# Spectral mixing with a gated causal unit on one core: set-up reordered, the filter worked up in four parts, the first batch loaded by two queues

## Chip, cores, metric

One core of one Trainium2 chip, one program of 11040 instructions, no loop left at run time. The metric is the device time of one execution in microseconds (us). Before the change it is 417.4 us, the median of three runs (417.29 to 417.82).

## What is computed

The reference, cut to its core. `x` is (8, 3200, 256) float32, the filter (1601, 256) in a real and an imaginary part, `K` is 5.

```python
X = np.fft.rfft(x, axis=1)
F = (filt_r + 1j * filt_i)[None, :, :]
y = np.fft.irfft(X * F, n=3200, axis=1)
...
xp = np.concatenate([zeros(B, K - 1, D), y], axis=1)
gate_pre = sum(conv_w[k] * xp[:, k:k + S, :] for k in range(K))
gate = 1.0 / (1.0 + np.exp(-gate_pre))
out = (gate * (y @ w_val)) @ w_out
```

## The kernel before

**The transform.** A sequence of 3200 is taken as 128 x 25 (L = 128, R = 25), and both directions are matrix products on TensorE. The 256 channels are cut into 52 groups of five (the last overlaps its neighbour), since 25 x 5 = 125 fills the partitions. The groups are cut into eight chunks of 6 or 7 (`CH`, NF = 8). With 8 batches there are 64 chunks, and one step G of the main loop (L496) starts one of them: step G runs the first stage of chunk G, and later stages of earlier chunks.

**The stages of a chunk.** `permute` (L95) reorders the chunk's channels from the loaded batch `xb` into `xpb`: on ScalarE (L105), or for odd chunks of batches 1 and later on GpSimd (L103). `s1` (L343) multiplies with the 128-point table `cf_t` on TensorE (L348), and VectorE copies the result to `sob` (L351). `s2` (L354), one step later, multiplies with the 25-point tables (L360 to L363), ScalarE copies to `xsb` (L365), and VectorE multiplies with the worked-up filter `fr_t`, `fm_t` (L376 to L379). `inva` (L383, two steps later still) starts the inverse. It is the last stage that works on chunks of groups.

**The stages of a batch.** From eleven steps after a batch's first chunk, `invb` (L403) finishes the inverse in seven pieces. With the first of them GpSimd copies a few columns of `yt` to the place where the causal convolution looks back (L423, L425). Two steps later `conv` (L427) runs the convolution as matmuls (L434) and needs that copy; `val` (L444) and `outp` (L462) follow, and SyncE (SP) stores the result (L478). So for batch 0: `s1` of chunk 13 and the first `conv` are in the same step, G = 13.

**Loading x.** `load_x(b, r)` (L81) loads residue r of batch b as float32 rows of 1 KB which the transfer turns into bf16. Because 3200 rows don't divide evenly it takes two transfers for each r but r = 0: 49 a batch, all issued by GpSimd (L88). Three buffers `xb` turn round. Batch 0 is issued in the set-up (L170), the others from a queue in the main loop (L485, L502): at step G the queue is worked off up to entry (G + 8) x 25/8, which at G = 0 is the whole of batch 1. Right behind it comes `load_w` (L506), eight transfers of the two weight matrices, and then batch 2. GpSimd's `permute` instructions and its `yt` copies stand in the same in-order stream, between those issues.

**Set-up (L109 to L324).** Tables are made by VectorE and ScalarE. SP issues four loads of the filter: `gd` (rows used as they are) and `gh` (rows that have to be reversed), for the real (i = 0) and the imaginary part (i = 1), then two small ones of `cw`, from which VectorE makes `dg_t` (L320). Then, first for i = 0 and after that for i = 1: `turn` copies `gd` into `gp` (L247 or L249); `gh` is reversed by float32 matmuls with `rev` (L262), three times two, and turned into `gp` as well; 52 matmuls (L272) with ScalarE or VectorE copies give `ft`; 50 matmuls for both parts together (25 each, L293) with copies (L307, L309, L310) fill `fr_t` and `fm_t`. All 52 groups go through each stage together. ScalarE does the copies of i = 0 up to `ft`, VectorE those of i = 1. The main loop's matmuls stand behind all of this in TensorE's order.

**Order.** The program fixes what depends on what. A planner orders each engine's instructions by the order in the program and by its own estimate of when inputs are there; on the chip each engine then works in that order and waits where an input is late. PSUM is four tiles, `ps`, that turn round over all of these stages.

Of the kernel before, what the change touches and what calls it, by code (L numbers as in the profile page):

```python
# [11 lines left out]
I32 = mybir.dt.int32  # L12
# [18 lines left out]
def kernel(  # L31
# [48 lines left out]

    def load_x(b, r):  # L81
        xt = xb[b % NX]
        na = min(L, -(-(S - L * r) // R))
        for a0, a1, s in ((0, na, L * r), (na, L, L * r + R * na - S)):
            if a1 > a0:
                src = bass.AP(tensor=x.tensor, offset=x.offset + (b * S + s) * D,
                              ap=[[R * D, a1 - a0], [1, D]])
                nc.gpsimd.dma_start(out=xt[a0:a1, r, :], in_=src)  # L88
# [6 lines left out]
    def permute(b, c):  # L95
        g0, nd = CH[c]
        xt = xb[b % NX]
        xp = xpb[(NF * b + c) % NP]
        for i0, i1, d0 in split(g0, nd):
            dst = xp[:, i0:i1, :].rearrange("p g (r j) -> p g r j", j=J)  # L100
            src = xt[:, :, d0:d0 + J * (i1 - i0)].rearrange("p r (g j) -> p g r j", j=J)
            if c % 2 and b > 0:
                nc.gpsimd.tensor_copy(dst, src)  # L103
            else:
                nc.scalar.activation(dst, src, AF.Copy)  # L105

    C2, S2, SN2 = (tb_t[0:P2, i].rearrange("p k j -> p (k j)") for i in (0, 1, 2))

    with tc.tile_pool(name="gen", bufs=1) as g1, tc.tile_pool(name="gen2", bufs=2) as g2:  # L109

        def floormod(src_ap, divisor):
            shp = list(src_ap.shape)
            divi = g2.tile(shp, I32, name=f"fm_i{shp[1]}")
            bak = g2.tile(shp, FP32, name=f"fm_b{shp[1]}")
            q = g2.tile(shp, FP32, name=f"fm_q{shp[1]}")
            cm = g2.tile(shp, FP32, name=f"fm_c{shp[1]}")
            nc.vector.tensor_scalar(divi[...], src_ap, 1.0 / float(divisor), None,
                                    op0=ALU.mult)
            nc.vector.tensor_copy(bak[...], divi[...])
            nc.vector.scalar_tensor_tensor(q[...], bak[...], -float(divisor), src_ap,  # L120
                                           op0=ALU.mult, op1=ALU.add)
            nc.vector.tensor_scalar(cm[...], q[...], float(divisor) - 0.5, None,
                                    op0=ALU.is_ge)
            nc.vector.scalar_tensor_tensor(q[...], cm[...], -float(divisor), q[...],
                                           op0=ALU.mult, op1=ALU.add)
            nc.vector.tensor_scalar(cm[...], q[...], -0.5, None, op0=ALU.is_lt)
            nc.vector.scalar_tensor_tensor(q[...], cm[...], float(divisor), q[...],
                                           op0=ALU.mult, op1=ALU.add)
            return q

        def iota(shape, pattern, base, cm, name):
            t = g1.tile(shape, FP32, name=name)
            nc.gpsimd.iota(t[...], pattern=pattern, base=base, channel_multiplier=cm,
                           allow_small_or_imprecise_dtypes=True)
            return t

        nc.vector.memset(b_npi[:, :], -PI)
        pcol = iota([128, 1], [[0, 1]], 0, 1, "pcol")
        kc = iota([128, 2, 64], [[-1, 2], [1, 64]], 1, 0, "kc")
        kt = iota([128, 2 * R], [[1, 2 * R]], 0, 0, "kt")  # L140
        kt65 = iota([128, 65], [[1, 65]], 0, 0, "kt65")
        q64 = iota([128, 1], [[0, 1]], 64, -1, "q64")
        ident = g1.tile([128, 128], FP32, name="ident")
        nc.vector.memset(ident[:, :], 1.0)
        nc.gpsimd.affine_select(out=ident[:, :], in_=ident[:, :], pattern=[[1, 128]],
                                compare_op=ALU.is_equal, fill=0.0, base=0,
                                channel_multiplier=-1)
        ac = g1.tile([128, 1], FP32, name="ac")
        nc.vector.memset(ac[...], 2.0)
        for i in (63, 64):  # L150
            nc.gpsimd.affine_select(out=ac[...], in_=ac[...], pattern=[[0, 1]],
                                    compare_op=ALU.not_equal, fill=1.0, base=-i,
                                    channel_multiplier=1)

        gd, gh, gp = [], [], []
        for i, f in enumerate((filt_r, filt_i)):
            g = g1.tile([65, 13, D], FP32, name=f"gd{i}")
            nc.sync.dma_start(
                out=g[...],
                in_=bass.AP(tensor=f.tensor, offset=f.offset,  # L160
                            ap=[[D, 65], [L * D, 13], [1, D]]))
            h = g1.tile([65, 12, D], FP32, name=f"gh{i}")
            nc.sync.dma_start(
                out=h[...],
                in_=bass.AP(tensor=f.tensor, offset=f.offset + 64 * D,
                            ap=[[D, 65], [L * D, 12], [1, D]]))
            gd.append(g)
            gh.append(h)
            gp.append(g1.tile([65, ND, R, J], BF16, name=f"gp{i}"))
        for r in range(R):  # L170
            load_x(0, r)
        for t in sob:
            nc.vector.memset(t[:, :, 0:1], 0.0)
            nc.vector.memset(t[:, :, SW - 1:SW], 0.0)
        for t in xsb:
            nc.vector.memset(t[:, :, :, 65:W], 0.0)

        pr = g1.tile([128, 128], FP32, name="pr")
        nc.vector.tensor_scalar(pr[...], kc[...].rearrange("p b k -> p (b k)"),
                                pcol[:, 0:1], None, op0=ALU.mult)  # L180
        nc.vector.tensor_scalar(pr[:, 0:65], pr[:, 0:65], 0.75 * L, None, op0=ALU.add)
        q = floormod(pr[...], L)
        nc.scalar.activation(cf_t[:, :], q[...], AF.Sin, bias=b_npi[:, 0:1],
                             scale=2.0 * PI / L)

        jp = g1.tile([128, 1], FP32, name="jp")
        nc.vector.tensor_copy(jp[...], floormod(pcol[...], J)[...])
        rp = g1.tile([128, 1], FP32, name="rp")
        nc.vector.tensor_tensor(rp[...], pcol[...], jp[...], op=ALU.subtract)
        nc.vector.tensor_scalar(rp[...], rp[...], 1.0 / J, None, op0=ALU.mult)  # L190
        mk = g1.tile([128, J], FP32, name="mk")
        nc.vector.tensor_scalar(mk[...], kt[:, 0:J], jp[:, 0:1], None, op0=ALU.is_equal)

        ph = g1.tile([128, 2 * R], FP32, name="ph")
        nc.vector.tensor_scalar(ph[:, 0:R], kt[:, 0:R], rp[:, 0:1], 4.0, op0=ALU.mult,
                                op1=ALU.mult)
        nc.vector.tensor_scalar(ph[:, R:2 * R], ph[:, 0:R], 3.0 * R, None, op0=ALU.add)
        qp = floormod(ph[...], 4 * R)
        sc = g1.tile([128, 2, R], FP32, name="sc")
        nc.scalar.activation(sc[...].rearrange("p c k -> p (c k)"), qp[...], AF.Sin,  # L200
                             bias=b_npi[:, 0:1], scale=2.0 * PI / (4 * R))

        def expand(dst, src, n):
            nc.vector.tensor_tensor(dst, src.unsqueeze(2).to_broadcast((128, n, J)),
                                    mk[...].unsqueeze(1).to_broadcast((128, n, J)),
                                    op=ALU.mult)

        expand(tb_t[:, 2], sc[:, 0], R)
        expand(tb_t[:, 0], sc[:, 1], R)
        nc.vector.tensor_scalar(tb_t[:, 1], tb_t[:, 2], -1.0, None, op0=ALU.mult)  # L210

        m3 = g1.tile([128, 1], FP32, name="m3")
        hi = g1.tile([128, 1], FP32, name="hi")
        nc.vector.tensor_scalar(hi[...], rp[...], 12.5, None, op0=ALU.is_ge)
        nc.vector.tensor_scalar(m3[...], rp[...], -2.0, 37.0, op0=ALU.mult, op1=ALU.add)
        nc.vector.tensor_tensor(m3[...], m3[...], hi[...], op=ALU.mult)
        nc.vector.tensor_tensor(m3[...], m3[...], rp[...], op=ALU.add)
        nc.vector.tensor_scalar(m3[...], m3[...], 3.0, None, op0=ALU.mult)
        m3q = floormod(m3[...], R)
        xr = g1.tile([128, 2, R], FP32, name="xr")  # L220
        for h in range(2):
            nc.vector.tensor_scalar(xr[:, h, :], kt[:, 0:R], m3q[:, 0:1], None,
                                    op0=ALU.is_equal)
# [332 lines left out]
```

## Time and profile before

| what | us |
|---|---|
| median of the runs | 417.4 |
| the profiled execution's own time | 416.61 |
| span of that execution | 414.9 |
| first `s1` matmul (L348) starts | 61.47 |
| `s1` of chunk 3 | 67.75 |
| `s1` of chunk 8 | 80.42 |
| first GpSimd `permute` (L103, chunk 9) | 88.97 |
| `s1` of chunk 9 | 89.95 |
| first `yt` copy on GpSimd (L423, L425) | 108.23 |
| first `conv` matmul (L434) | 109.33 |
| from one batch's `s1` to the next in the later batches | 40.3 |

Engine busy shares over the span: PE (TensorE matmul) 86%, DVE (VectorE) 73%, ACT (ScalarE) 66%, POOL (GpSimd) 60%. They average over a set-up, a start and a steady part that differ, so the stretches have to be read one by one: which wait ends last there. Starts are us from the span's start; an entry in brackets behind a timeline row is the time for which the engine sat idle before it, and what ended that.

### The profile page before, as it was taken

The numbers are of one execution on the slowest core, as the hardware profiler recorded it, in microseconds if no ns is written. First come the engines' busy times: TensorE is split into PE (matmuls) and PEld (weight loads), VectorE is DVE, ScalarE is ACT, GpSimd is POOL, SyncE is SP. The second block draws the span as 40 slices with busy tenths as digits, with TensorE's granted clock in tenths as the row PEclk, the third lists the DMA queues.
The fourth block names the chain that finished last, engine by engine and source line by source line (L and its number), as shares of the span: only waits on it lengthen the run. The fifth ranks groups of instructions, "written<-read, shape, count | busy, mean of one in ns | idle before, by whom it ended". The sixth has DMA issues, their size and how long they took to land.

```text
span 414.9 us, 11040 instructions
## 1 busy us (share of the span) xinstructions
PE 357.3 (86%) x4628; PEld 241.1 (58%) x4659; DVE 304.7 (73%) x465; ACT 274.4 (66%) x338; POOL 249.2 (60%) x471
## 2 busy tenths in 40 slices
PE   0688868938598999899999999999999999999994
PEld 0154466626366676667666756666766666666552
DVE  5235578948577798779977888788878887874454
ACT  2442246828567787778777877787778777766762
POOL 5599999899999998899994979210021002000000
PEclk9999999979699999999999999999999999999998
DMA  7976667556458766776683757231222122213334
GB/s 147 183 95 70 64 61 66 57 54 63 47 55 165 148 124 107 157 147 127 108 161 104 138 97 156 92 120 45 107 86 92 52 103 80 90 52 141 128 153 164
DMA packets 48951, 43.65 MB, mean 105 GB/s; under 512 B 12628, under 2 KB 41734, under 8 KB 48902
## 3 DMA queue, kind: packets, MB, share of 16 engines
q0 software_dynamic: 36224, 13.41, 31.5%
q1 hardware_dynamic: 12678, 29.55, 19.8%
q8 instruction: 36, 0.59, 0.6%
q14 instruction: 13, 0.11, 0.1%
HBM read 30.07 MB, written 26.21 MB: 136 GB/s over the span
## 4 chain that ended last, share of the span: by engine, by line
PE 52%; POOL 21%; DVE 13%; DMA 6%; issue 4%; ACT 3%; DVEq 0%; ACTq 0%; POOLq 0%
POOL xb L88 18%; PE ps L434 10%; PE ps L451 8%; PE ps L394 8%; PE ps L468 7%; DMA xb<-in_x_dram 6%; PE ps L416 5%; DVE o L473 4%; PE ps L348 4%; DVE za L376 2%; PE ps L360 2%; DVE zb L378 2%; PE ps L363 2%; PE ps L362 2%; PE ps L361 2%
## 5 line engine op out<-in xcount | busy, mean ns | idle before, releaser
L88 POOL DMA_DIRECT2D xb<-in_x_dram x392 | 203.9, 551 | 18.0 <-DMA xb<-in_x_dram 11.7
L439 ACT ACTIVATE gt<-ps 128x1024 bf16<-128x1024 f32 (+1 forms) x56 | 52.2, 933 | 60.4 <-PE ps L434 58.0
L456 DVE TENSOR_TENSOR gv<-ps,gt 128x1024 bf16<-128x1024 f32 (+1 forms) x56 | 62.1, 1109 | 37.9 <-PE ps L451 28.8
L351 DVE CAST sob<-ps 125x768 bf16<-125x768 f32 x64 | 65.4, 1022 | 29.7 <-PE ps L348 29.0
L103 POOL COPY xpb<-xb 128x875 bf16<-128x875 bf16 (+2 forms) x35 | 30.3, 869 | 72.1 <-PE ps L348 72.1
L434 PE MATMUL ps<-yt,dg_t 64*64 64x512 bf16 (+1 forms) x1120 | 66.6, 362 | 3.0 <-POOL yt L425 2.8
L365 ACT ACTIVATE xsb<-ps 125x780 bf16<-125x780 f32 x64 | 56.5, 883 | 15.0 <-PE ps L363 14.1
L394 PEld LDWEIGHTS <-z 125*64 125x64 bf16 x1664 | 49.9, 112 | 26.6 <-issue 25.7
L394 PE MATMUL ps<-tb_t,z 125*64 125x125 f16 x1664 | 60.7, 223 | 0.4 <-PE ps L363 0.4
L399 ACT ACTIVATE u<-ps 128x750 bf16<-128x750 f32 (+2 forms) x72 | 57.1, 793 | 2.8 <-PE ps L394 0.7
L418 ACT ACTIVATE yt<-ps 128x1024 bf16<-128x1024 f32 (+1 forms) x56 | 52.2, 932 | 4.5 <-PE ps L416 4.5
L468 PE MATMUL ps<-wo_t,gv 128*128 128x256 bf16 x400 | 52.8, 273 | 1.1 <-DVE gv L456 1.1
L451 PE MATMUL ps<-yt,wv_t 128*128 128x512 bf16 (+1 forms) x193 | 50.8, 352 | 1.9 <-DMA xb<-in_x_dram 0.3
L348 PE MATMUL ps<-cf_t,xpb 128*125 128x128 f16 x416 | 37.2, 231 | 14.9 <-POOL xpb L103 8.9
L468 PEld LDWEIGHTS <-gv 128*128 128x128 bf16 x400 | 38.9, 98 | 14.3 <-DVE gv L456 1.5
L376 DVE TENSOR_TENSOR za<-xsb,fr_t 125x792 bf16<-125x792 bf16 x64 | 40.4, 631 | 5.4 <-ACT xsb L365 4.7
L434 PEld LDWEIGHTS <-dg_t 64*64 64x64 bf16 x1120 | 28.4, 107 | 27.0 <-issue 14.5
L379 DVE TENSOR_TENSOR z<-za,zb 125x792 bf16<-125x792 bf16 x64 | 43.3, 676 | 1.1
L348 PEld LDWEIGHTS <-xpb 128*125 128x125 bf16 x416 | 32.0, 145 | 17.8 <-POOL xpb L103 9.4
L378 DVE TENSOR_TENSOR zb<-xsb,fm_t 125x792 bf16<-125x792 bf16 x64 | 40.5, 632 | 0.0
L416 PE MATMUL ps<-ci_t,u 128*128 128x128 f16 x400 | 33.4, 222 | 7.6 <-ACT u L399 7.1
L473 DVE COPY o<-ps 128x1024 f32<-128x1024 f32 (+1 forms) x32 | 36.8, 1150 | 2.3 <-PE ps L468 2.3
(92 smaller groups left out, 367.7 us busy)
## 6 DMA issues: line engine op xcount, KB each, us to landing
out_dram<-o SPq DMA_DIRECT2D x32, 512.0 KB, 3.1
out_dram<-o SPq DMA_DIRECT2D x24, 384.0 KB, 2.3
gd<-in_filt_r_dram SPq DMA_DIRECT2D x1, 845.0 KB
gd<-in_filt_i_dram SPq DMA_DIRECT2D x1, 845.0 KB
gh<-in_filt_r_dram SPq DMA_DIRECT2D x1, 780.0 KB
gh<-in_filt_i_dram SPq DMA_DIRECT2D x1, 780.0 KB
xb<-in_x_dram POOLq DMA_DIRECT2D x8, 64.0 KB, 2.8
xb<-in_x_dram POOLq DMA_DIRECT2D x8, 61.5 KB, 2.6
```

The source lines that it names most:

```text
L88: nc.gpsimd.dma_start(out=xt[a0:a1, r, :], in_=src)
L348: nc.tensor.matmul(ps[0:P2, 128 * i:128 * i + 128], lhsT=xp[:, i, :], rhs=cf_t[:, :], start=True, stop=True)
L351: nc.vector.tensor_copy(so[0:P2, 0:nd, 1:SW - 1], ps[0:P2, 0:nd * 128].rearrange("p (g k) -> p g k", g=nd))
L365: nc.scalar.activation(xs[0:P2, :, 0:nd, 0:65], ps[0:P2, :].rearrange("p (c n) -> p c n", c=2)[:, :, 0:65 * nd] .rearrange("p c (g k) -> p ...
L394: nc.tensor.matmul(ps[lo:lo + 64, o:o + P2], lhsT=z[0:P2, blk, i, s0:s0 + 64], rhs=tab, start=first, stop=not first)
L399: nc.scalar.activation(u[:, :, d0:d0 + J * (i1 - i0)].rearrange("p r (g j) -> p r g j", j=J), pv[:, i0:i1, :].rearrange("p g (r j) -> p r ...
L416: nc.tensor.matmul(ps[:, o:o + L], lhsT=u[:, r, 128 * dh:128 * dh + 128], rhs=cw_[:, sh:sh + L], start=True, stop=True)
L434: nc.tensor.matmul(ps[64 * dh:64 * dh + 64, 512 * r:512 * r + np_ * L], lhsT=dg_t[rows, dh, k, :], rhs=y[rows, dh, p0 + k:p0 + k + np_, :] ...
L451: nc.tensor.matmul(ps[:, 512 * eh:512 * eh + np_ * L], lhsT=wv_t[:, dh, 128 * eh:128 * eh + 128], rhs=y[:, dh, H + p0:H + p0 + np_, :], st ...
L456: nc.vector.tensor_tensor(gv[:, :, 0:np_ * L], ps[:, :].rearrange("p (h n) -> p h n", h=2)[:, :, 0:np_ * L], g[:, :, 0:np_ * L], op=ALU.mult)
L468: nc.tensor.matmul(ps[:, D * a:D * a + D], lhsT=gv[:, eh, L * a:L * a + L], rhs=wo_t[:, eh, :], start=(eh == 0), stop=(eh == 1))
L473: nc.vector.tensor_copy(o[:, 0:np_, :].rearrange("p a d -> p (a d)"), ps[:, 0:np_ * D])
```

## The change

Nothing changes in the arithmetic, but for the reversal in bf16 and the order.

1. **Two queues for batch 0.** GpSimd loads the odd residues as before (24 transfers). The even ones are loaded by SP (`load_plain`), in float32, into a new tile `x0`, cut so that the row counts divide well: 33 transfers. `permute` for batch 0 takes the even residues from `x0` and the odd ones from `xb`, two instructions for a piece: ScalarE for the even ones, VectorE for the odd ones of chunks 0 and 1, ScalarE for those of chunks 2 to 7.
2. **The reversal in bf16.** `gh` is loaded by GpSimd, cast to bf16 on the way (two transfers ahead of the x loads), and `rev` is bf16. SP's order is now `gd` twice, 33 pieces of x, `cw` twice.
3. **The filter in four parts.** `turn` runs for both i, the reversed part first. `filt(h)` takes 13 groups through both later stages, for both i: 26 matmuls, copies, and 2 x 25 matmuls with three copies a target. `filt(0)` is in the set-up, `filt(1)` to `filt(3)` follow the `s2` of steps 0 to 2. The `fr_t` copies go from VectorE to ScalarE.
4. **The order around it.** `permute` runs three steps ahead rather than two; batch 1 is issued whole at step 0; `load_w` moves to step 1; the queue of the other batches starts at batch 2 with the bound G x 25/8 (the same place in the stream of loads as before). The set-up's tiles are given back at step 3, `x0` at step 6, and the pools that take their place are opened there.

```diff
+    def load_plain(r):
+        for a0, a1, s in pieces(r):
+            n = a1 - a0
+            k = max(i for i in range(1, 17) if n % i == 0)
+            cut = n if n <= 16 or n // k <= 17 else n // 16 * 16
+            for o, m in ((0, cut), (cut, n - cut)):
+                if m:
+                    nc.sync.dma_start(out=x0[a0 + o:a0 + o + m, r // 2, :],
+                                      in_=xrows(0, s + R * o, m))
...
+            cols = slice(d0, d0 + J * (i1 - i0))
+            if b == 0:
+                nc.scalar.activation(
+                    dst[:, :, 0:R:2, :],
+                    x0[:, :, cols].rearrange("p r (g j) -> p g r j", j=J), AF.Copy)
+                src = xt[:, 1:R:2, cols].rearrange("p r (g j) -> p g r j", j=J)
+                if c < 2:
+                    nc.vector.tensor_copy(dst[:, :, 1:R:2, :], src)
+                else:
+                    nc.scalar.activation(dst[:, :, 1:R:2, :], src, AF.Copy)
+                continue
...
-            h = g1.tile([65, 12, D], FP32, name=f"gh{i}")
-            nc.sync.dma_start(
+        h = g1.tile([65, 12, D], BF16, name=f"gh{i}")
+        nc.gpsimd.dma_start(
...
+    for r in range(R):
+        if r % 2:
             load_x(0, r)
+        else:
+            load_plain(r)
...
-        rev = g1.tile([128, 65], FP32, name="rev")
+    rev = g1.tile([128, 65], BF16, name="rev")
...
+    for h in range(3):
         for i in range(2):
+            ps = psum()
+            for s in range(2):
+                nc.tensor.matmul(ps[0:65, 512 * s:512 * s + 512], lhsT=rev[0:65, :],
+                                 rhs=gh[i][:, 4 * h + 2 * s:4 * h + 2 * s + 2, :],
+                                 start=True, stop=True)
+            turn(i, 13 + 4 * h, 4, ps[0:65, :].rearrange("p (m d) -> p m d", m=4))
+    for i in range(2):
+        turn(i, 0, 13, gd[i])
+
+    def filt(h):
+        for i in range(2):
+            qv = gp[i][...].rearrange("p g m j -> p g (m j)")
+            t1 = g2.tile([128, 65, 13], BF16, name=f"ft{i}")
+            ps = psum()
+            for s, (o, n) in enumerate(((0, 6), (6, 7))):
+                for a in range(n):
+                    nc.tensor.matmul(ps[0:P2, 512 * s + 65 * a:512 * s + 65 * a + 65],
+                                     lhsT=qv[:, 13 * h + o + a, :],
+                                     rhs=idb[0:65, 0:65], start=True, stop=True)
...
+            ps = psum()
+            for u0, nu, nt, c0 in ((0, 13, 3, 0), (13, 2, 3, 512), (15, 10, 2, 590)):
+                n = 13 * nt
+                for uu in range(nu):
...
+                    nc.tensor.matmul(ps[0:P2, c0 + n * uu:c0 + n * (uu + 1)],
+                                     lhsT=exf[0:P2, w0:w0 + P2],
+                                     rhs=t1[0:P2, u:u + R * (nt - 1) + 1:R, :],
                                      start=True, stop=True)
...
+                if i == 0:
+                    nc.scalar.activation(dst_ap(fr_t[0:P2]), pv, AF.Copy)
+                else:
+                    nc.scalar.activation(dst_ap(fm_t[0:P2, 0]), pv, AF.Copy, scale=-1.0)
+                    nc.vector.tensor_copy(dst_ap(fm_t[0:P2, 1]), pv)
...
+    filt(0)
...
-    queue = [(b, r) for b in range(1, B) for r in range(R)]
+    queue = [(b, r) for b in range(2, B) for r in range(R)]
...
             permute(0, 1)
-        if G + 2 < NS:
-            permute(*divmod(G + 2, NF))
-        want = min(len(queue), (G + 8) * R // NF)
+            permute(0, 2)
+            for r in range(R):
+                load_x(1, r)
+        if G + 3 < NS:
+            permute(*divmod(G + 3, NF))
+        if G == 1:
+            load_w()
+        want = min(len(queue), G * R // NF)
...
-        if G == 0:
-            load_w()
+        if G == 3:
+            gstack.close()
...
+        if G == NF - 2:
+            fstack.close()
...
+        if G < 3:
+            filt(G + 1)
```

## The prediction

> **What bounds the kernel now.** I read the page's shares of the chain that ended last first, then that chain in order of time, then TensorE's timeline where the chain names another engine, then transfers and durations for the prices.
>
> ```profile
> PE 52%; POOL 21%; DVE 13%; DMA 6%; issue 4%; ACT 3%; DVEq 0%; ACTq 0%; POOLq 0%
> ```
>
> POOL's 21% and the 6% of DMA don't lie spread over the run. In order of time (start, duration, what):
>
> ```profile
> 1.98 9.50 DMA xb<-in_x_dram
> ...
> 11.76 7.36 DMA xb<-in_x_dram
> ...
> 19.40 6.35 DMA xb<-in_x_dram
> ...
> 26.03 38.04 POOL xb L88 x74
> ...
> 88.97 0.93 POOL xpb L103
> ...
> 108.41 1.76 POOL yt L425 x2
> ```
>
> Up to 110 us the chain is GpSimd's stream alone: three waits for landings, then 74 issues without a gap, 38.04 / 74 = 0.514 us each (25 of batch 0, 49 of batch 1), the weights, batch 2, and in between its `permute` and `yt` copies. The set-up's matmuls aren't on it. TensorE shows where it feels this:
>
> ```profile
> 61.47 1.69 PE L348 MATMUL ps<-cf_t,xpb 128*125 128x128 f16 x13 [0.73 <-DVE fm_t L310]
> ...
> 89.95 1.01 PE L348 MATMUL ps<-cf_t,xpb 128*125 128x128 f16 x7 [6.66 <-POOL xpb L103]
> ...
> 109.33 0.58 PE L434 MATMUL ps<-yt,dg_t 64*64 64x512 bf16 x1 [2.76 <-POOL yt L425]
> ```
>
> TensorE starts the loop at 61.47, gets to chunk 9, idles 6.66 us for GpSimd's `permute`, and idles again before the first `conv` for the `yt` copy. So the whole set-up could end several us later at no cost, and the last wait before the steady part (40.3 us a batch) is GpSimd's.
>
> **Part 1, the first batch by two queues.** Before 26 us the transfer engines bound, after it the issuing:
>
> ```profile
> 2.60:26.00 23.40, 10.76 (x13) 2.75 (x13) 9.20 (x55) 8.45 (x11) 13.89 (x25) 1.00 0.98 174
> 26.00:39.00 13.00, 11.17 (x75) 8.94 (x76) 6.51 (x17) 4.45 (x9) 12.97 (x26) 1.00 0.59 61
> ```
>
> (Columns: stretch, busy of PE, PEld, DVE, ACT, POOL, clock, DMA share, GB/s.) From 26 us POOL is full (12.97 of 13) and the transfers at 0.59. There, 25 issues leave GpSimd's stream: 25 x 0.514 = 12.9 us at most. Batch 0's last issue is now at 26.03 + 12.85 = 38.9. When is it afterwards? The transfer queues up to 24 us:
>
> ```profile
> q1 hardware_dynamic: 4512, 3.33, 68.5%
> q0 software_dynamic: 1671, 0.64, 21.3%
> ```
>
> A packet of SP's queue took 0.685 x 16 x 24 / 4512 = 58 ns, one of GpSimd's 0.213 x 384 / 1671 = 49 ns, with 1671 / (0.64 MB / 512 B) = 1.34 packets a row. Afterwards GpSimd's queue carries 1560 rows of `gh` and 1536 of x: 3096 x 1.34 x 49 ns = 203 us; SP's 1690 of `gd` and 1664 of x: 3354 x 58 ns = 195 us. Together 398 / 16 = 24.9 us, at 0.98 busy 25.4, from 2.6 us on: all is in at 28.0, whichever queue gets the larger share, if the sixteen engines are evenly loaded. `cw`'s 1280 packets (4.6 us of all engines) now come behind this. The last issue comes about 2.3 us ahead of its landing (the median of L88), at 25.7. Evenness isn't given: 65 partitions of the filter and pieces of 6 to 128 rows don't divide by 16. I take 27.5. Bounds: not before 2.0 + 2 x 0.9 + 24 x 0.514 = 16.1 (issue alone, a `gh` issue priced as the 256-run `wv` row, 0.88), nor much after 34 (6 us of uneven load). **Gain on GpSimd's stream: 38.9 - 27.5 = 11.4 us** (4.9 to 22.8).
>
> The Trainium skill (DMA: Bandwidth & Descriptors, section "Issuing engines are not separate DMA queues") says that issuing from several engines at once saves only the sequencer's issue time, usually small beside the transfer. By that the move would buy next to nothing and the time would stay at 417.4; the row of 26 to 39 us, POOL full and transfers at 0.59, speaks against it for this kernel, and that of 2.6 to 26 us for it.
>
> SP's 33 issues (0.33 us each on the stores' rows, 11 us) delay only `cw`; SP has no store before 126 us.
>
> **Part 4, the order on GpSimd.** Per step the same issues stand ahead of the same copies but for this: chunk 9's `permute` comes behind 29 loads of batch 2, not 35 (3.1 us earlier), and then 38 rather than 32 stand between it and the `yt` copy (3.1 us later). `load_w` stays between batches 1 and 2. So `permute` of chunk 9 moves from 88.97 to 74.5, `yt` from 108.23 to 96.8, and the first `conv`, 1.1 us behind, from 109.33 to 97.9: again 11.4.
>
> **Parts 2 and 3 on TensorE.** They pay only if they bring TensorE to `conv` before 97.9. Prices:
>
> ```profile
> L262 PE MATMUL ps<-gh,rev 65*65 65x512 f32 x24 | 21.2, 1064 | 0.7 <-DMA gh<-in_filt_r_dram 0.5 <-DVE fr_t L307 0.2
> L272 PE MATMUL ps<-idb,gp 65*125 65x65 f16 x104 | 11.5, 295 | 2.5 <-DVE gp L249 1.3 <-ACT gp L247 1.1
> ```
>
> The reversal's 24 records go to 12 (bf16, 512 columns; by L361, 0.38 for 455 columns, about 0.43): 21.2 to 5.2 us. The bf16 load of `gh` costs GpSimd two issues, counted above. The second stage goes from 50 matmuls to 200 of 39 or 26 columns: nearest row L272 (same 125-column weights, 65 columns), 5.76 / 52 = 0.111 us; bounds 0.081 (L348 later in the run) and 0.134 (L293). A part is 76 x 0.111 = 8.4 us, four are 33.7; before, the two stages took 104 x 0.111 + 50 x 0.134 = 18.2. So TensorE saves 16 and pays 15.5; what moves is that `s1` doesn't wait for all of it.
>
> `gh` lands near 11 and 18 us (half of all packets share the engines), `gp` for i = 1 is ready after 0.9 + 3 x 1.3 + 2.0 of VectorE, about 25; i = 0 some 5 us sooner. From 25: 33.7 - 4.2 + `s1` three times 0.9 + `s2` twice 1.6 = 35.4, and 3 us for hand-overs (1.3 idle at L272's two rows): **`s1` of chunk 3 at 63.4** (67.75 before). From there to `conv` it was 12.7 us for five steps, 13 for five more and 1.3: arrival 90.4, **7.5 us before GpSimd lets it go**. That covers the copies too: a part costs ScalarE some 4.9 us (1.24 `ft`, 3.6 for six `fr_t`/`fm_t` copies by the 468-, 416- and 208-element rows), with `permute` and `xsb` 6.9 a step against TensorE's 10.8; VectorE 6. Splitting batch 0's `permute` costs ScalarE 0.25 us a chunk (0.83 for 750 elements, 0.30 for 125: two halves pay the fixed part twice), some 1.5 us, covered as well. Without that cover each us late at `conv` beyond 97.9 is a us of the end.
>
> **Sum.** 416.61 for the profiled execution (span 414.9 and 1.7 around it) - 11.4 = 405.2; it lies 0.8 below the median 417.4, so 406.0 on the median's scale.
>
> **Rivals.**
> B, the interleaved filter becomes the bound. `dg_t` waits for `cw`, now behind 33 pieces (landing perhaps 43 us); if it stands ahead of the filter's copies in VectorE's order, TensorE's i = 1 half waits too, or matmuls cost 0.134 and hand-overs double. `s1` of chunk 3 then at 74 to 80, `conv` at 101 to 107: 2 to 8 us gained, 409 to 415, say 412. For: 200 matmuls. Against: 7.5 us of cover.
>
> C, GpSimd gets through batch 0 at about 22 us. `yt` at 91.3, `conv` 92.4, still behind TensorE's 90.4: gain 17, 400.5. Against: the 0.98.
>
> D, slower. ScalarE works in order, and `permute` of chunks 0 to 2 may stand ahead of the first filter copies:
>
> ```profile
> 40.93 3.24 ACT L105 ACTIVATE xpb<-xb 128x750 bf16<-128x750 bf16 x4 [7.86 <-DMA xb<-in_x_dram]
> ```
>
> That wait stood there before, with L309 queued behind and not yet ready. If x lands at X and the filter waits, chunk 3 is at X + 3 + 39, `conv` at X + 69: slower than 109.33 from X = 40 on (before: 40.9). X = 46 gives 423. Against: 28 by the sum above.
>
> E, no change, 417.4: the transfer engines, not the issuing, set batch 0's landing, so that GpSimd's stream is as late as before.
>
> **Chances.** Forecast 0.53 (its own range 403 to 409), B 0.20, C 0.13, D 0.09, E 0.05. Range 400 to 414: it takes in C's and most of B's value and leaves out D and E. A measurement here tells 0.2% (0.8 us) from no change. Faster: forecast, C and nearly all of B, 0.85; within 0.2%: 0.05; slower 0.10.
>
> **What would show it.** Right: GpSimd's last issue of batch 0 near 27.5, `permute` of chunk 9 near 74.5, `yt` near 97 with TensorE idle before `conv` for it; L262's successor near 0.43 us a matmul; `s1` of chunk 3 near 63 with TensorE full before it; 40.3 us a batch as before. Wrong: `conv` started by anything but GpSimd (B), DVE waiting for `cw` ahead of filter copies (B), ACT waiting for x with filter copies behind it (D), batch 0's last issue beyond 34 (E).

## The result, and the profile after

After the change the kernel takes 422.42 us (median of four runs, 422.38 to 423.48); the kernel before took 417.35 beside it (four runs, 417.03 to 417.82). The ratio is 1.0127, 95% interval 1.0108 to 1.0145: **slower by 5.1 us**, where 406.0 was forecast. The profiled execution's span grew from 414.9 to 420.7, by 5.8.

In the profile after the change `load_x` issues are L92, GpSimd's `permute` is L128, ScalarE's and VectorE's for batch 0 L117, L122 and L124; the reversal is L294, the two stages of a part L308 and L324 with their copies at L315, L317 and L338 to L341, `s1` L376, `s2` L388 to L391, the border copies of `yt` L451 and L453, `conv` L462. The shares of the chain that ended last look as before (PE 55%, POOL 19%). GpSimd's timeline doesn't (start, duration, instruction, idle time before it and what ended that):

```profile
17.21 0.55 POOL L92 DMA_DIRECT2D xb<-in_x_dram  x1 [9.88 <-DMA gh<-in_filt_r_dram]
21.73 34.59 POOL L92 DMA_DIRECT2D xb<-in_x_dram  x66 [3.97 <-DMA gh<-in_filt_i_dram]
56.31 0.77 POOL L364 DMA_DIRECT2D wv_t<-in_moe_w_val_dram  x1
...
61.30 15.02 POOL L92 DMA_DIRECT2D xb<-in_x_dram  x29
86.55 1.34 POOL L128 COPY xpb<-xb 128x875 bf16<-128x875 bf16 x1 [10.23 <-PE ps L376]
...
110.43 1.56 POOL L453 COPY yt<-yt 128x508 bf16<-128x508 bf16 x2
...
155.14 1.16 POOL L453 COPY yt<-yt 128x508 bf16<-128x508 bf16 x2
```

GpSimd reaches the weights at 56.31, 7.8 us earlier than before (64.07), and has the 29 loads ahead of chunk 9's `permute` done at 76.3. Then it stands for 10.23 us, released by TensorE's `s1` of chunk 5: four buffers `xpb` turn round, so that `permute` can't start until TensorE has used up the one it writes to, and every load and copy behind it stands too. The lead is spent: the first border copies come at 110.43, later than before the change (108.28 in the same view).

What TensorE is doing meanwhile, from its timeline:

```profile
21.50 4.42 PE L294 MATMUL ps<-gh,rev 65*65 65x512 bf16 x10 [3.51 <-DMA gh<-in_filt_i_dram]
26.21 1.59 PE L308 MATMUL ps<-idb,gp 65*125 65x65 f16 x13 [0.29 <-ACT gp L281]
28.95 2.74 PE L324 MATMUL ps<-ft,ex 125*125 125x39 bf16 x25 [1.15 <-ACT ft L315]
31.54 1.57 PE L308 MATMUL ps<-idb,gp 65*125 65x65 f16 x13
34.43 2.84 PE L324 MATMUL ps<-ft,ex 125*125 125x39 bf16 x25 [1.32 <-DVE ft L317]
41.31 0.90 PE L376 MATMUL ps<-cf_t,xpb 128*125 128x128 f16 x6 [4.04 <-ACT xpb L117]
...
76.92 2.85 PE L324 MATMUL ps<-ft,ex 125*125 125x39 bf16 x25 [1.87 <-DVE ft L317]
79.61 0.99 PE L376 MATMUL ps<-cf_t,xpb 128*125 128x128 f16 x7
```

The two stages of one half of a part stand right behind each other, so TensorE waits at each second stage for the `ft` copy of the first: 1.15, 1.32, 1.14, 1.32, 1.31, 1.32, 1.21 and 1.87 over the four parts, 10.6 us together. Before the first `s1` it waits 4.04 us more for the `permute` of batch 0, and ScalarE's timeline shows why:

```profile
31.73 1.07 ACT L338 ACTIVATE fr_t<-ps 125x507 bf16<-125x507 f32 x3 [2.83 <-PE ps L324]
37.31 0.62 ACT L340 ACTIVATE fm_t<-ps 125x507 bf16<-125x507 f32 x1 [4.51 <-PE ps L324]
...
39.71 1.09 ACT L124 ACTIVATE xpb<-xb 128x360 bf16<-128x360 bf16 x2
40.67 2.57 ACT L117 ACTIVATE xpb<-x 128x390 bf16<-128x390 f32 x5
```

Its first `permute` pieces stand behind the first part's `fr_t` and `fm_t` copies, 4.51 us of which it waited for TensorE itself. `s1` of chunk 3 starts at 79.61 (before 67.75). From there, `s1` starts of some chunks in the two traces:

| `s1` of chunk | before | after | later by |
|---|---|---|---|
| 3 | 67.75 | 79.61 | 11.9 |
| 9 | 89.95 | 96.98 | 7.0 |
| 16 | 126.44 | 125.64 | -0.8 |
| 21 | 151.35 | 150.56 | -0.8 |
| 22 | 155.96 | 160.10 | 4.1 |
| 28 | 188.35 | 194.74 | 6.4 |
| 32 | 208.37 | 214.01 | 5.6 |
| 63 | 362.81 | 368.60 | 5.8 |

So the late start isn't what one sees at the end: by chunk 16 it is made good, because before the change TensorE waited for GpSimd in that stretch (6.66, 0.63, 1.64 and 2.76 us from chunk 9 to the first `conv`). The loss opens between chunks 21 and 22. In the kernel before, GpSimd's border copies of batch 1 were earlier and held nothing:

```profile
149.83 1.17 POOL L425 COPY yt<-yt 128x508 bf16<-128x508 bf16 x2
```

After the change they run at 155.14 and TensorE's `conv` waits 3.12 us for them:

```profile
155.81 2.89 PE L462 MATMUL ps<-yt,dg_t 64*64 64x512 bf16 x20 [3.12 <-POOL yt L453]
```

The wait isn't its whole price: the twenty matmuls behind it took 2.89 us, against 1.27 for the same twenty before the change (from 153.41), and the granted clock was 0.50 from 156 to 159 us. That makes 4.7 of the 4.9 us lost there. The steady 40.3 us a batch is unchanged (208.37 to 248.67 and 214.01 to 254.46), so what is lost there stays lost.

### The profile page after: what moved, and what is told of

The parts are those of the page before. It is cut to its first block, busy times and chain, and to the rows that moved or that the text cites. A ratio compares the mean times of both kernels' runs of the same rounds, so it can differ in the third digit from the quotient of the medians.

```text
span 420.7 us, 11354 instructions
## 1 busy us (share of the span) xinstructions
PE 354.7 (84%) x4766; PEld 251.8 (60%) x4797; DVE 302.0 (72%) x463; ACT 278.1 (66%) x361; POOL 237.0 (56%) x448
## 4 chain that ended last, share of the span: by engine, by line
PE 55%; POOL 19%; DVE 11%; DMA 6%; issue 5%; ACT 4%; ACTq 0%; DVEq 0%; POOLq 0%
POOL xb L92 16%; PE ps L462 10%; PE ps L422 7%; PE ps L479 7%; PE ps L496 6%; PE ps L444 5%; PE ps L376 5%; DMA gh<-in_filt_i_dram 4%; PE ps L324 4%; DVE o L501 4%; PE ps L388 2%; DVE za L404 2%; PE ps L391 2%; PE ps L390 2%; PE ps L389 2%
## 5 line engine op out<-in xcount | busy, mean ns | idle before, releaser
L92 POOL DMA_DIRECT2D xb<-in_x_dram x367 | 189.4, 533 | 20.3 <-DMA gh<-in_filt_r_dram 9.9
L128 POOL COPY xpb<-xb 128x875 bf16<-128x875 bf16 (+2 forms) x35 | 30.2, 867 | 87.8 <-PE ps L376 87.8
L462 PE MATMUL ps<-yt,dg_t 64*64 64x512 bf16 (+1 forms) x1120 | 66.9, 362 | 3.9 <-POOL yt L453 3.9
L462 PEld LDWEIGHTS <-dg_t 64*64 64x64 bf16 x1120 | 28.6, 107 | 31.1 <-issue 18.3
L404 DVE TENSOR_TENSOR za<-xsb,fr_t 125x792 bf16<-125x792 bf16 x64 | 42.8, 669 | 5.6 <-ACT xsb L393 4.8
L376 PE MATMUL ps<-cf_t,xpb 128*125 128x128 f16 x416 | 37.0, 230 | 10.3 <-DVE o L501 5.9
L376 PEld LDWEIGHTS <-xpb 128*125 128x125 bf16 x416 | 31.4, 144 | 12.5 <-issue 7.2
```

The costliest lines, as they stand in the source:

```text
L92: nc.gpsimd.dma_start(out=xb[b % NX][a0:a1, r, :], in_=xrows(b, s, a1 - a0))
L376: nc.tensor.matmul(ps[0:P2, 128 * i:128 * i + 128], lhsT=xp[:, i, :], rhs=cf_t[:, :], start=True, stop=True)
L462: nc.tensor.matmul(ps[64 * dh:64 * dh + 64, 512 * r:512 * r + np_ * L], lhsT=dg_t[rows, dh, k, :], rhs=y[rows, dh, p0 + k:p0 + k + np_, :] ...
```

## The experiments

Two causes offered themselves: **T**, TensorE's late start holds GpSimd at chunk 9's `permute`, and GpSimd, with its stream of issues late, then holds TensorE at the border copies; and **O**, the order of the loads against the copies in GpSimd's stream is at fault by itself. The median of the kernel before was 416.4, 417.3, 417.7 and 420.4 on the chips of the four sets of runs, so the comparisons go by ratios to it. The expectations of `e1`, `e3` and `e10` put chunk 3 of the changed kernel at 83: that is where chunk 4 starts (83.23, six matmuls; chunk 3 has seven). Chunk 3 starts at 79.61, and the runs are held against that here.

### Border copies on VectorE

In the changed kernel (`e1`), and alone in the kernel before (`e2`):

```diff
-            nc.gpsimd.memset(y[:, :, 0:H, 0:1], 0.0)
+            nc.vector.memset(y[:, :, 0:H, 0:1], 0.0)
...
-                nc.gpsimd.tensor_copy(y[:, dh, 0:H, 1:L], y[:, dh, R:R + H, 0:L - 1])
+                nc.vector.tensor_copy(y[:, dh, 0:H, 1:L], y[:, dh, R:R + H, 0:L - 1])
```

> The changed kernel with the yt copies on VectorE instead of GpSimd. Changed kernel: 422.4 us, s1 of chunk 22 at 160.10 (before: 155.96), GpSimd's second yt copy at 155.14. Theory T (TensorE's late start holds GpSimd's stream, and its yt copy of batch 1 then holds TensorE 5 us): that wait goes, the late start stays; s1 of chunk 3 still near 83, chunk 22 near 155.3, 416.5 to 418. Theory O (the planner put too many loads ahead of that copy, whatever TensorE does): the same here, 417. Theory N (the 5 us come from elsewhere, transfers of batch 3 for instance): 421 to 423.

> The kernel before with the yt copies on VectorE. If GpSimd's copy is what the first conv waits for at 109.33 (2.76 us of idle TensorE), that wait goes: 413.5 to 416 of 417.4. If TensorE loses it again at the next wait: 417.

`e1`: 415.79 us, ratio 0.9956 (0.9915 to 0.9997). `e2`: 412.24 us, ratio 0.9868 (0.9802 to 0.9934), somewhat better than expected. In `e1` `s1` of chunk 22 follows that of chunk 21 after 4.53 us, as before the change (155.16 and 150.63), but GpSimd still stands behind TensorE:

```profile
85.98 1.10 POOL L128 COPY xpb<-xb 128x875 bf16<-128x875 bf16 x1 [10.94 <-PE ps L376]
```

Both theories had this result. The border copies are where the loss reaches the end: without them on GpSimd the changed kernel is 7 us faster. That doesn't tell why they are late, and with them moved in both, the changed kernel is still behind (415.8 against 412.2).

### The two halves' first stages back to back

`filt` does the first stage of both halves and then the second stage of both, so that the copy of one half is hidden by the matmuls of the other. Nothing else changes (`e3`):

```diff
     def filt(h):
+        t1s = []
         for i in range(2):
...
+            t1s.append(t1)
+        for i in range(2):
+            t1 = t1s[i]
             ps = psum()
             for u0, nu, nt, c0 in ((0, 13, 3, 0), (13, 2, 3, 512), (15, 10, 2, 590)):
```

> The changed kernel with the two first stages (i = 0 and 1) of each filter part back to back, then the two second stages, so that TensorE needn't wait for the ft copies (10.6 us of waits before s1 of chunk 3 in the changed kernel). Theory T: s1 of chunk 3 at 74 to 77 instead of 83.2, GpSimd's wait ahead of chunk 9's permute down from 10.2 to 2 to 4 us, its yt copy of batch 1 about 7 earlier, 414 to 417. Theory O: chunk 3 earlier as well, but the yt copy of batch 1 stays where the loads ahead of it put it, 421 to 422.

410.42 us, ratio 0.9842 (0.9767 to 0.9918): 12 us better than the changed kernel, more than T expected. TensorE's and GpSimd's timelines of `e3`:

```profile
38.48 0.90 PE L380 MATMUL ps<-cf_t,xpb 128*125 128x128 f16 x6 [4.04 <-ACT xpb L117]
39.18 2.93 PE L309 MATMUL ps<-idb,gp 65*125 65x65 f16 x26
41.92 5.49 PE L328 MATMUL ps<-ft,ex 125*125 125x39 bf16 x50
...
68.25 0.99 PE L380 MATMUL ps<-cf_t,xpb 128*125 128x128 f16 x7
```

```profile
60.98 14.99 POOL L92 DMA_DIRECT2D xb<-in_x_dram  x29
75.96 1.18 POOL L128 COPY xpb<-xb 128x875 bf16<-128x875 bf16 x1
...
99.61 1.17 POOL L457 COPY yt<-yt 128x508 bf16<-128x508 bf16 x2
```

26 and 50 matmuls now follow each other without a bracket. `s1` of chunk 3 is at 68.25, 11.4 us earlier than in the changed kernel, about the 10.6 us of its hand-overs; chunk 9's `permute` runs right behind its loads, with no wait, and the first border copies come 10.8 us earlier. The loads and copies stand in the same order, so O falls as the cause of this delay, and T stands for it. The stream's order still has a price of its own: TensorE loses 3.6 us more from chunk 21 to 22 than in the kernel before (8.2 against 4.6), `e5` below gains by moving the copies though nothing holds GpSimd at chunk 9, and so did the kernel before (`e2`). The 4.04 us ahead of the first `s1` are still there.

### Loads later in GpSimd's stream

If GpSimd's idle time at chunk 9's `permute` could be moved to a harmless place, the changed kernel should lose less (`e4`):

```diff
-        want = min(len(queue), G * R // NF)
+        want = min(len(queue), max(0, G - 4) * R // NF)
```

> The changed kernel with the queue of loads of batches 2 to 7 four steps later (bound (G - 4) x 25/8), which leaves 114 x loads rather than 139 ahead of the first yt copy and 185 rather than 211 ahead of the second. T and O: GpSimd's second yt copy comes before TensorE needs it, s1 of chunk 22 near 155.3, 416.5 to 418. N: no change, 422. If the loads now come too late for the next batch, the first permute of batch 2 or 3 waits for x and the time is above 422.

429.39 us, ratio 1.0278 (1.0211 to 1.0345): a miss, and to the other side. Fewer loads stand ahead of the `permute`, and GpSimd only waits longer:

```profile
86.65 0.93 POOL L128 COPY xpb<-xb 128x875 bf16<-128x875 bf16 x1 [22.96 <-PE ps L376]
```

The `permute` runs when TensorE lets it, as in the changed kernel. The border copies of batch 1 do come earlier (152.02) and TensorE no longer waits for them, but those of batch 2 come at 204.25 behind the loads that were put off, and there TensorE waits 6.42 us. An issue left out of an idle stretch has to be made in a busy one.

### Both, and each part undone

`e5` is `e3` with the border copies on VectorE. `e6`, `e7` and `e8` start from `e3`: `e6` gives all of batch 0 to GpSimd again (part 1 undone), `e7` loads `gh` as float32 by SP and reverses in float32 (part 2), `e8` puts all four parts ahead of the loop (the interleaving of part 3).

```diff
 # e6
-            if c % 2:
+            if c % 2 and b > 0:
...
-        if r % 2:
-            load_x(0, r)
-        else:
-            load_plain(r)
+        load_x(0, r)
 # e7
-        h = g1.tile([65, 12, D], BF16, name=f"gh{i}")
-        nc.gpsimd.dma_start(
+        h = g1.tile([65, 12, D], FP32, name=f"gh{i}")
+        nc.sync.dma_start(
...
-    rev = g1.tile([128, 65], BF16, name="rev")
+    rev = g1.tile([128, 65], FP32, name="rev")
 # e8
-    filt(0)
+    for h in range(4):
+        filt(h)
...
-        if G < 3:
-            filt(G + 1)
```

> The changed kernel with both edits: filter stages back to back for the two i, and yt copies on VectorE. With the first edit alone: 410.4 us, first conv at about 100.8 behind GpSimd's yt copy, further waits for yt copies around s1 of chunks 22 and 28. Theory T (once TensorE isn't late, GpSimd's stream sets the start again, through the yt copies above all): those waits go, 2.5 us at the first conv, 3.7 and 2.8 later: 401 to 405. If the waits are only replaced by others: 409 to 411.

> Part 1 undone in the kernel with the stages back to back (410.4): all of batch 0 loaded by GpSimd, permute reads xb alone. Theory T: 25 issues of 0.514 us go back into GpSimd's stream, 12.9 us; permute of chunk 9 from 76 to 87 to 89, first yt copy from 99.7 to 111 to 113; batch 0's x lands at 45 or later, s1 of chunk 0 at 46 to 48 instead of 38.5; 420 to 424. Rival (transfer engines set batch 0's landing, the second queue buys nothing): s1 of chunk 0 within 2 us of 38.5 and 409 to 412.

> Part 2 undone in the kernel with the stages back to back (410.4): gh loaded by SP in float32, rev in float32, 24 matmul records of about 0.87 us instead of 12 of 0.43. GpSimd loses its two gh issues and the wait behind them, TensorE gets 15.6 us of work ahead of the first filter part. Theory T: s1 of chunk 3 at 78 to 84 instead of 68.25, so that GpSimd's chunk-9 permute waits for TensorE again: 416 to 421. If TensorE's work in the set-up is covered by GpSimd's stream: 408 to 411.

> Part 3's interleaving undone in the kernel with the stages back to back (410.4): still four parts, but all of them ahead of the main loop. The matmuls are the same, s1 of chunk 0 moves from 38.5 to about 60 to 62, chunk 3 stays at 66 to 69, since TensorE loses its 4 us wait for x. Theory T (only TensorE's arrival at chunk 3 counts): 408 to 412. If the early start of the first chunks is what pays: 415 or more.

| kernel | us | ratio to before | `s1` of chunk 3 | `permute` of chunk 9 |
|---|---|---|---|---|
| changed kernel | 422.42 | 1.0127 (1.0108 to 1.0145) | 79.61 | 86.55 |
| `e3` | 410.42 | 0.9842 (0.9767 to 0.9918) | 68.25 | 75.96 |
| `e5` | 405.48 | 0.9707 (0.9654 to 0.9761) | 68.59 | 76.20 |
| `e6` | 420.29 | 1.0086 (1.0050 to 1.0122) | 73.71 | 88.49 |
| `e7` | 422.08 | 1.0116 (1.0062 to 1.0170) | 83.98 | 90.45 |
| `e8` | 411.41 | 0.9831 (0.9762 to 0.9900) | 66.25 | 75.79 |

`e5` lies just above what T gave, 405.48 against 401 to 405, `e6` within it. **Part 1** is worth (1.0086 - 0.9842) x 417.4 = 10.2 us once the hand-overs are out of the way. In `e6` TensorE is ready and GpSimd's stream is late:

```profile
83.93 4.56 POOL L92 DMA_DIRECT2D xb<-in_x_dram  x9 [1.87 <-issue]
88.49 1.34 POOL L118 COPY xpb<-xb 128x875 bf16<-128x875 bf16 x1
```

Without part 1 the `permute` stands where it stood in the kernel before (88.97), with no wait for TensorE ahead of it. **Part 2** is worth 11.4 us; `e7` came out just above what was expected. There the other engine is late, as in the changed kernel:

```profile
24.55 17.33 PE L294 MATMUL ps<-gh,rev 65*65 65x512 f32 x20 [6.64 <-DMA gh<-in_filt_i_dram]
```

```profile
90.45 1.34 POOL L128 COPY xpb<-xb 128x875 bf16<-128x875 bf16 x1 [17.90 <-PE ps L380]
```

**Part 3's interleaving** is worth nothing that can be told: `e8` comes to chunk 3 within 2 us of `e3` and takes the same time, as T had it. A late TensorE at chunk 3 costs, but not us for us: `e7` loses in another place of the set-up than the changed kernel, comes to chunk 3 later (83.98 against 79.61) and to chunk 9's `permute` later (90.45 against 86.55), and takes the same time. In its trace chunk 22 follows chunk 21 after 6.3 us, in the changed kernel's after 9.5: what is lost at the border copies depends on where GpSimd and TensorE stand to each other there, not on chunk 3 alone.

### All parts ahead of the loop, border copies on VectorE, and dense matmuls ahead of the filter

`e9` puts `e8` and the border copies together, `e10` is the changed kernel once more beside it. In `e11` and `e12` matmuls of 128x512 whose output nothing reads are added to `e5` and `e9`, because the filter's matmuls run at a slower pace than those of the later chunks:

```diff
+    def warm(n):
+        pw = psum()
+        for a in range(n):
+            nc.tensor.matmul(pw[:, 0:512], lhsT=wt[:, 0:128], rhs=wt[:, :],
+                             start=True, stop=True)
...
+    warm(12)
     nc.vector.memset(fr_t[:, :, 65:W], 0.0)
...
+            if h == 0 and i == 0:
+                warm(10)
```

> All four parts of the filter ahead of the loop (as in e8) with the border copies of yt on VectorE (as in e5). T (TensorE's arrival at chunk 3 and, behind it, GpSimd's stream set the end, and moving the border copies takes the second of GpSimd's two holds away): e8's 411.4 less what the copies were worth on e3 (410.4 to 405.5, 4.9) gives 406.5; first stage of chunk 3 near 66, 402 to 407. N (the order of the four parts matters in itself once GpSimd's hold at the border copies is gone): more than 3 us away from e5's 405.5 on either side.

> The changed kernel once more, unaltered, beside the others on the same chip: 421 to 424, first stage of chunk 3 at 83, the wait of GpSimd at the permute of chunk 9 near 10 us.

> e5 with 12 matmuls of 128x512 on a zeroed bf16 tile ahead of the reversal and 10 more in TensorE's wait between the two halves of the filter; nothing reads their output. In e5 the first stage of a part takes 2.93 us for 26 matmuls and its second 5.49 for 50, and the same second-stage matmuls of the chunks run at 0.53 us until 72 us and at 0.36 from then on. W (the slow pace is TensorE's clock, and dense work ahead brings it up before the filter): the two stages of each part in some 1.9 and 3.6 us, first stage of chunk 3 near 58 to 62, end 399 to 404. S (the slow pace belongs to the shapes, or dense work ahead doesn't last through the filter's small matmuls): stages as in e5, chunk 3 at 68 to 69, end 404 to 407; the added matmuls lie in waits and cost under 1 us.

> e9 with the 22 matmuls of e11 (12 ahead of the reversal, 10 between the halves; nothing reads their output). In e11 the first part ran at twice e5's pace, then TensorE waited 4.35 us for x and the pace and the granted clock stayed at half until 71 us. W (the clock was lost to the gap and not to the small matmuls): without the gap all four parts run at e11's first pace, some 6 us each with the evacuations, chunk 3 at 48 to 56; the end is then GpSimd's, 398 to 403, because the permute of chunk 9 has no wait to lose any more. S (the small matmuls themselves let the clock fall): the later parts at 8.1 us again, chunk 3 at 60 to 66, 401 to 405.

`e9`: 403.24 us, ratio 0.9658 (0.9607 to 0.9709). `e10`: 422.18 us, 1.0100 (1.0047 to 1.0154), with chunk 3 at 79.67 and GpSimd's wait at 10.95. `e11`: 404.04 us, 0.9669 (0.9625 to 0.9713). `e12`: 404.61 us, 0.9675 (0.9623 to 0.9728). `e9` beats the kernel before by 14 us, within T's range and less than N's 3 us from `e5`; that the added matmuls gain anything can't be told. In `e11` the first stage of the first part does run faster, but little after it, and chunk 3 comes at 65.83, between W and S (PE timeline, then 10 us stretches with busy time of PE, PEld, DVE, ACT, POOL, granted clock, DMA share, GB/s):

```profile
24.60 0.94 PE L321 MATMUL ps<-idb,gp 65*125 65x65 f16 x13 [0.56 <-ACT gp L291]
25.76 0.94 PE L321 MATMUL ps<-idb,gp 65*125 65x65 f16 x13 [0.22 <-DVE gp L293]
26.69 5.04 PE L340 MATMUL ps<-ft,ex 125*125 125x39 bf16 x50
36.07 0.90 PE L392 MATMUL ps<-cf_t,xpb 128*125 128x128 f16 x6 [4.35 <-ACT xpb L117]
36.76 2.93 PE L321 MATMUL ps<-idb,gp 65*125 65x65 f16 x26
39.50 5.49 PE L340 MATMUL ps<-ft,ex 125*125 125x39 bf16 x50
```

```profile
20.00:30.00 10.00, 8.54 (x76) 6.18 (x74) 4.95 (x8) 4.09 (x9) 8.11 (x16) 0.86 0.83 161
...
40.00:50.00 10.00, 10.00 (x88) 9.61 (x87) 4.23 (x7) 5.21 (x11) 9.98 (x21) 0.50 0.65 67
50.00:60.00 10.00, 10.00 (x85) 9.40 (x85) 4.24 (x8) 5.24 (x11) 10.00 (x19) 0.50 0.63 61
```

The first stage takes 0.94 us a half (1.57 in the changed kernel), but the second, right behind it, 5.04 against `e5`'s 5.49: the pace was lost there, ahead of the 4.35 us wait and not in it, so the expectation of `e12` read `e11` too kindly. The granted clock falls to 0.50 and stays there with PE busy 10.00 of 10 us. In `e12`, where no wait for x interrupts the filter, the clock was 0.50 from 30 us to 60 as well, and 26 first-stage matmuls took 2.95 us already at 24.52. W holds for one stage of the first part, S for the rest.

## Why the prediction was wrong, step by step

**What bounds the kernel: right.** GpSimd's stream set the end before: its border copies moved away gave 5.5 us (`e2`).

**Part 1: right in kind, 11.4 us was too much.** Batch 0's last issue was forecast at 27.5; from 21.73 its remaining 17 issues at 34.59 / 66 = 0.524 us put it at 30.6, a gain of 8.3, and at the weights it is 7.8. The term that was off is the landing of `gh`, forecast near 11 and 18 us: GpSimd's ninth and tenth transfers waited until 17.21 and 21.73 for the first and second to finish. SP's 33 issues took 26.8 us (1.81 to 28.60) and not 11, at no cost, since only `cw` stands behind them. In `e3` and `e6` the part is worth its 10 us.

**Part 4, "the same issues ahead of the same copies": the order held, the conclusion didn't.** `permute` of chunk 9 was forecast at 74.5; its loads were done at 76.3. It ran at 86.55. The prediction counted what stands ahead of it in its own stream and never asked what else it waits for. It is the buffer that TensorE's `s1` of chunk 5 hands back, and the answer is in the profile after: 10.23 us for PE. By the prediction's own 63.4 that `s1` would have ended near 69.7 (5.65 us from chunk 3 to 5 as before the change, and 0.6), 4.8 us ahead of the 74.5. It started at 85.78, 16.7 us later than by that reckoning, and 16.7 less 4.8 puts `permute` at 86.4, where it ran. This meeting of the two engines comes before the one at `conv`, and the sum had no term for it.

**Parts 2 and 3: this step failed.** The prices of the matmuls were right: the reversal's 10 records took 4.42 us (0.44 each, forecast 0.43), a part's 76 matmuls come to 8.4 to 8.7. `s1` of chunk 3 was forecast at 63.4 and came at 79.61, 16.2 us late. What failed is what stands ahead of them and between them, the hand-overs first (the table adds up to 16.1):

| term | forecast | measured | off by |
|---|---|---|---|
| start of the first part | 25 | 26.2 | 1.2 |
| matmuls done before it (i = 0's first half) | 4.2 | 0 | 4.2 |
| hand-overs in four parts | 3 | 10.6 | 7.6 |
| wait for `permute` ahead of the first `s1` | 0 | 4.0 | 4.0 |
| `s1` three times, `s2` twice | 5.9 | 5.0 | -0.9 |

Before the change all 52 groups went through a stage together, and the second stage (L293) waited for `ft` twice, 1.33 and 1.44 us. Cut into four parts it waits eight times, at about the same price each. The prediction cut the filter and left the number of waits as it was. Nor did i = 0 get ahead: the reversal takes i = 0 and i = 1 in turn, so ten of its twelve records stood behind the second `gh` (21.50). And "the copies are covered" on ScalarE held for their sum, not for the order: three copies that wait for TensorE stood ahead of the `permute` that TensorE waited for.

**The cover of 7.5 us was too large.** The prediction took 27.0 us from chunk 3 to `conv`: 12.7, 13 and 1.3. In the trace before, chunk 8 to chunk 13 takes 24.86 us, and without its waits for GpSimd (6.66, 0.63 and 1.64) 15.9, not 13. So the cover was some 4.6 us. With that, 16.2 us late less 4.6 puts `conv` 11.6 beyond 97.9, at 109.5; it came at 111.49, of which 0.62 is a wait for GpSimd. In `e1`, without GpSimd's copies, it came at 110.74 with no wait. So at the first `conv` TensorE's own lateness had used up the whole gain, and the sum would have been near 418 to 420, no gain.

**The sum ended too early.** It was closed at the first `conv`, as if GpSimd's stream met TensorE there for the last time. It meets it at each batch's border copies, and the changed kernel went from 0.8 us ahead at chunk 21 to 5.6 behind at chunk 32, at the copies of batches 1 and 2 (table of chunks). In `e1`, without these copies on GpSimd, chunk 22 comes as soon after chunk 21 as before the change; `e4` loses at batch 2's. That GpSimd is late there because it stood behind TensorE at chunk 9 is shown by `e3`, where it doesn't stand: batch 1's border copies come at 144.27 instead of 155.14, earlier by 10.9, about the wait. Against the kernel before, the wait isn't the whole account. There chunk 9's `permute` ran 2.4 us later than after the change (88.97), and batch 1's copies still came 5.3 us earlier (149.83). Between the two GpSimd's stream has 109 loads after the change and 100 before: nine at 0.52 are 4.7 us, and pauses of 1.56 and 1.35 come on top. Part 4 had booked six of these loads as 3.1 us less ahead of that `permute` and 3.1 more behind it. That cancels only while the `permute` doesn't wait; here GpSimd stood idle ahead of it, and the loads came behind. So T and O have a share each in the loss at batch 1. The loss from chunk 21 to 22 shrinks only a little (8.2 us, 9.5 in the changed kernel, 4.6 before), since TensorE is earlier too and GpSimd is the bound of this stretch again; that is why `e5` and `e9` gain once more by moving the copies.

**The rivals.** B named the place, the interleaved filter becomes the bound, and its chunk 3 at 74 to 80 holds 79.61. That is partly luck: it doubled the hand-overs to 6 us, where they were 10.6, and let the matmuls cost 0.134 us, where they stayed at 0.11. Its end of 409 to 415, still a gain, was wrong, since from chunk 3 it took the same 27 us to `conv` and ended there as well. D was the case on the slow side, but its mechanism, `permute` ahead of the filter's copies waiting for x, didn't occur: the order was the reverse. C and E fell with part 1. `dg_t` cost nothing.

**Left open.** Part 4 was not undone by itself, so its share in the loss is counted from the trace and not measured; `e4` is the one run that shifts its order. Chunk 28 loses another 1.8 us, where VectorE's `za` took 2.02 us instead of 0.56 while GpSimd copied (190.26 to 193.34); that was not tried by itself.

## What to carry to other kernels

When work is cut into n parts, multiply its hand-overs by n as well, and put an independent stage between a producer and its reader: that alone was worth 12 us here, while the interleaving itself was worth nothing that could be told. An engine that both issues loads and copies for others is a stream with two ends: for every copy in it ask what it waits for, because whatever stands behind it waits too, and issues put off from an idle stretch cost in a busy one (`e4`). Follow a delay through every place where the two engines meet, from the first to the last: here there was one ahead of the place where the sum was closed, and more behind it.

## What the runs showed of the hardware that was not expected

**TensorE's pace.** The second-stage matmuls of 39 columns took 0.11 us throughout. In `e3` PE was busy 37.83 of the 42.3 us from 26 to 68.3 and stayed at this pace; in `e5` an `s2` matmul of 455 columns took 0.59 us until 60 us and 0.36 from 73 us on. The page's clock reads 1.00 over that stretch in `e3` and 0.50 in `e11`, at the same durations (2.93 and 5.49 us in a part), so the 1.00 can't have been the clock in force; the trace of `e11`, where the clock went up first and fell, shows it. The Trainium skill (TensorE: Matmul & The Clock Gate, part 1) gives full speed after some 3.4 us of sustained activity; 20 us at PE 10.00 of 10 and 0.50 in `e11` disagree, for matmuls as small as these.

**A wait of TensorE cost more than its length.** Behind the wait of 3.12 us in the changed kernel and that of 6.42 in `e4`, twenty `conv` matmuls took 2.89 us instead of 1.27, with a granted clock of 0.50 in both stretches.

**A load that is issued first needn't land early.** `gh` by GpSimd's queue, two transfers of bf16 among SP's float32 pieces, released the queue at 17.2 and 21.7 us, though issued at 2 and 3.2.
